# Folding layer 2's DFT over columns twice, in a two-layer FNet and GLU kernel

## The chip, the core and the metric

The kernel runs on one core of one Trainium2 chip. The metric is the device time of one execution in microseconds (us), as the median of the runs shown. Engines are named as the profile names them: PE (TensorE matmuls), PEld (its weight loads), DVE (VectorE), ACT (ScalarE), POOL (GpSimd), SP (SyncE, which issues nearly all DMAs here).

## The reference

Four sublayers run one after the other on 2048 rows of 640 columns, in float32; the same two sublayers twice:

```python
def _A_ref(x, dft_seq_re, dft_seq_im, dft_hid_re, dft_hid_im):
    a = jnp.einsum("bsd,ed->bse", x, dft_hid_re)
    b = jnp.einsum("bsd,ed->bse", x, dft_hid_im)
    return jnp.einsum("ts,bse->bte", dft_seq_re, a) - jnp.einsum("ts,bse->bte", dft_seq_im, b)

def _B_ref(x, w_gate, w_up, w_down):
    g = jnp.einsum("bsd,df->bsf", x, w_gate)
    u = jnp.einsum("bsd,df->bsf", x, w_up)
    return jnp.einsum("bsf,fd->bsd", _sigmoid(g) * u, w_down)

x = A_x
x = x + _A_ref(_layernorm(x), ...)
x = x + _B_ref(_layernorm(x), B_w_gate, B_w_up, B_w_down)     # F = 1728
x = x + _A_ref(_layernorm(x), ...)
x = x + _B_ref(_layernorm(x), B_w_gate, B_w_up, B_w_down)
```

The Fourier tables are inputs, so the kernel may use their symmetries only if it tests on the chip that they have them.

## The kernel before, in words

All rows of x stay in SBUF. Wherever precision matters a float32 value is cut into two float16 parts, a high part (ACT, `activation` with Copy) and a residue (DVE), by `split`; a product is then three matmuls: high with high, high with low, low with high (`PASSES`).

**The Fourier part.** Rows lie in four quads (`GA` to `GD`), so that rows s, S - s, S/2 - s and S/2 + s stand in one place. `fold_columns` adds and subtracts column c and column 640 - c, into an even part `fe` of 321 columns (`EC`) and an odd part `fo` of 320 (`EH`). `fold_rows` applies the layer norm and folds two rows onto each other; `fold_join` joins the four quads into the sums for even (`EV`) and odd (`OD`) output rows and cuts them into parts "e" and "o". `sequence(i, tp)` is one step of 18 matmuls, the DFT over rows for quad i and parity tp, into three PSUM banks (three column tiles, `KT`: 128, 128 and 65 columns). `evict_sums` cuts these sums into the parts `z`. `hidden(q, ph)` and `hidden_middle` are the DFT over columns: `product` runs three matmuls for each of three tiles and both tables (18 in all), with 321 columns of the table `h` moving each time. Two banks hold its result. `evict_hidden` brings them out, `combine`, `join_hidden` and `add_hidden` unfold them and add them to x. The sequence step of layer 2 is called "he" (its first step's index), and "b0" is the first step of the gate block that follows.

**The gate blocks and the down products.** `gate_up` multiplies normalised and transposed rows by the gate and up weights (L1130). The later tiles use a scheme with seven products instead of eight (`seven`, `four`: L1174); the down product does likewise in seven stages (`stage`, `rest_stage`: L1430, L1411), and layer 1's first half runs plainly (`down`: L1316). The rows of a second half are prepared by `pair_apply`, `pair_combine`, `pair_parts` and DMA transposes (`pair_transpose`, L533).

**The tests.** `load_rows` and `test_rows` (and others like them, for columns and for the hidden tables) load 512 KB of a table into one of three rooms, fold it on DVE (L1509, L1511) and sum the squares on ACT (`square_rest`, L1481). 100 such tests are spread over the run: test n loads room n mod 3 at its slot, folds it two slots later, and squares 0.85 slots after that. The flag that they give decides at the end whether a general kernel has to run instead.

**The order.** `steps` is the list of PE's steps with planned lengths. `when(t, f)` puts a job ahead of the step that holds the planned time t; `run(u, ...)` puts jobs ahead of step u. Each engine then does its instructions in the order of issue. SBUF room is given by a fixed list of places (`PLACES`), one for each `take`; the eight PSUM banks go round in the order in which they are freed.

## Time and profile before

| | us |
|---|---|
| median of 3 runs | 1104.65 |
| lowest, highest | 1103.58, 1104.69 |
| profiled execution, own time | 1106.03 |
| its span | 1104.2 |
| PE busy | 1084.0 |
| DVE busy | 830.2 |
| ACT busy | 572.9 |
| POOL busy | 154.6 |

The profile is of one execution. Its span runs from the first to the last instruction; the execution's own time has a little around it. A group of the profile gives line, engine, operation, tiles and shape, how often it ran, its busy time and the mean length of one, and what ended the idle time of its engine before it. Matmuls are pipelined, so the listed length of one matmul is longer than the distance from one to the next; that distance is read from the length of a merged piece.

### The profile page before, as it was taken

What the parts mean: (1) busy time and instruction counts of PE and PEld (TensorE: products, weight loads), DVE (VectorE), ACT (ScalarE), POOL (GpSimd) and SP (SyncE); (2) the same over time, 40 slices, a digit from 0 to 9 for tenths busy, and PEclk for the clock granted to TensorE, in tenths of its full rate; (3) what the DMA queues carried; (4) which work ended last, traced back from release to release, by engine and by line L of the source; (5) the groups of instructions that cost most, each with busy time, mean ns of one, the idle gap of its engine ahead of it and who ended that gap; (6) DMA issues with size and microseconds to landing.
All of it is one profiled execution on the core that took longest, in us unless ns stands there. A gap on an engine that the chain in (4) does not pass through costs nothing.

```text
span 1104.2 us, 17528 instructions
## 1 busy us (share of the span) xinstructions
PE 1084.0 (98%) x6289; PEld 626.3 (57%) x6289; DVE 830.2 (75%) x1608; ACT 572.9 (52%) x1109; POOL 154.6 (14%) x250
## 2 busy tenths in 40 slices
PE   6999999999999999999999999999999999999997
PEld 3776444457774444457777844444677444444775
DVE  8996789868448999769887569895895356777962
ACT  7776547765315665555225544476761345555520
POOL 3110153312333151000110100012000010000010
PEclk9999999999999999999999999999999999999999
DMA  8414765366996877756742058645569856666521
GB/s 273 155 61 71 199 184 203 115 193 191 251 249 233 251 250 202 235 174 214 229 141 73 1 62 194 200 154 182 185 163 177 265 180 208 202 196 194 190 88 64
DMA packets 183079, 194.70 MB, mean 176 GB/s; under 512 B 76451, under 2 KB 145474, under 8 KB 182982
## 3 DMA queue, kind: packets, MB, share of 16 engines
q1 hardware_dynamic: 182342, 190.87, 58.8%
q0 software_dynamic: 640, 2.62, 0.6%
q8 instruction: 51, 0.84, 0.3%
q14 instruction: 46, 0.38, 0.1%
HBM read 145.29 MB, written 31.91 MB: 160 GB/s over the span
## 4 chain that ended last, share of the span: by engine, by line
PE 87%; DVE 8%; issue 2%; DMA 1%; ACT 1%; POOL 0%; SPq 0%; DVEq 0%; POOLq 0%; ACTq 0%
PE acc L1174 36%; PE acc L1430 17%; PE acc L1130 14%; PE acc L1316 8%; PE acc L922 4%; PE acc L1411 2%; PE acc L1283 2%; PE acc L834 2%; DVE big L642 1%; DMA big<-big 1%; DVE quad L424 1%; DVE big L239 1%; PE acc L796 1%; DVE big L1509 1%; DVE big L594 0%
## 5 line engine op out<-in xcount | busy, mean ns | idle before, releaser
L1174 PE MATMUL acc<-big 128*128 128x512 f16 x2160 | 467.8, 379 | 2.8 <-ACT big L1178 1.9
L1174 PEld LDWEIGHTS <-big 128*128 128x128 f16 x2160 | 211.3, 98 | 257.8 <-issue 3.5
L1430 PE MATMUL acc<-big 128*128 128x320 f16 x1512 | 213.2, 299 | 0.4 <-DVE big L1304 0.4
L1178 ACT ACTIVATE big<-acc 128x512 f32<-128x512 f32 x160 | 94.0, 593 | 191.9 <-PE acc L1174 167.5
L1430 PEld LDWEIGHTS <-big 128*128 128x128 f16 x1512 | 147.9, 98 | 58.5 <-issue 0.6
L1130 PE MATMUL acc<-big 128*128 128x512 f16 (+1 forms) x900 | 156.6, 336 | 0.0
L1130 PEld LDWEIGHTS <-big 128*128 128x128 f16 x900 | 87.9, 98 | 67.7 <-DVE big L239 0.2
L1481 ACT ACTIVATE big<-big 128x768 f32<-128x768 f32 (+6 forms) x106 | 79.0, 745 | 53.2 <-DVE big L1511 17.0
L1304 DVE SCALAR_TENSOR_TENSOR big<-acc,big 128x320 f32<-128x320 f32 x112 | 53.1, 485 | 53.7 <-PE acc L1411 27.2
L239 DVE SCALAR_TENSOR_TENSOR big<-big 128x640 f16<-128x640 f32 (+7 forms) x94 | 75.9, 830 | 22.5 <-ACT big L237 19.4
L1316 PE MATMUL acc<-big 128*128 128x320 f16 x656 | 89.3, 299 | 0.0
L1391 DVE TENSOR_TENSOR big<-big 128x512 f16<-128x512 f32 x126 | 85.3, 688 | 2.3 <-ACT big L1390 2.3
L1390 ACT ACTIVATE big<-big 128x512 f16<-128x512 f32 x126 | 74.0, 618 | 25.0 <-DVE big L1391 11.1
L237 ACT ACTIVATE big<-big 128x640 f16<-128x640 f32 (+9 forms) x94 | 63.8, 707 | 35.7 <-POOL big L1082 15.8
L1316 PEld LDWEIGHTS <-big 128*128 128x128 f16 x656 | 64.2, 98 | 25.1
L1224 DVE TENSOR_TENSOR big<-big,acc 128x512 f32<-128x512 f32 x40 | 27.3, 682 | 44.4 <-PE acc L1174 30.6
L516 ACT ACTIVATE big<-big 128x384 f16<-128x384 f32 (+2 forms) x56 | 36.0, 667 | 36.6 <-DVE big L501 17.2
L1181 ACT ACTIVATE big<-big 128x512 f32<-128x512 f32 x80 | 49.7, 622 | 9.7 <-DVE big L1224 6.6
L386 POOL DMA_INDIRECT out<-big,rows x8 | 8.6, 1070 | 310.9 <-DVE big L1304 173.5
L1509 DVE TENSOR_TENSOR big<-big 128x512 f32<-128x512 f32 x64 | 46.2, 722 | 5.9 <-DMA big<-in_ct 5.7
L1402 DVE TENSOR_TENSOR big<-big 128x512 f32<-128x512 f32 x72 | 50.1, 697 | 0.1
L439 POOL TENSOR_SCALAR rowt<-rowt 128x1 f32<-128x1 f32 x24 | 13.0, 540 | 242.4 <-ACT big L437 242.4
(199 smaller groups left out, 1230.2 us busy)
## 6 DMA issues: line engine op xcount, KB each, us to landing
big<-in_ct SPq DMA_DIRECT2D x256, 128.0 KB
big<-kept_f SPq DMA_DIRECT2D x63, 320.0 KB
big<-kept_S SPq DMA_DIRECT2D x33, 512.0 KB
big<-kept_w SPq DMA_DIRECT2D x33, 320.0 KB
big<-in_ct SPq DMA_DIRECT2D x32, 256.0 KB
big<-kept_G SPq DMA_DIRECT2D x21, 320.0 KB
kept_S<-big SPq DMA_DIRECT2D x13, 512.0 KB
big<-in_wg SPq DMA_DIRECT2D x19, 320.0 KB
```

Of the source, the lines that this page charges most:

```text
L237: nc.scalar.activation(dh, src, AF.Copy, scale=s)
L239: nc.vector.scalar_tensor_tensor(dl, src, s, dh, op0=OP.mult, op1=OP.subtract)
L1130: nc.tensor.matmul(ps, w[wp][:, d * P : (d + 1) * P], xt[:, xp, :], start=(d == 0 and wp == HI and xp == HI), stop=(d == ND - 1 and wp == LO))
L1174: nc.tensor.matmul(ps, wt, xt, start=start and n == 0, stop=n == len(todo) - 1, skip_group_check=not start)
L1178: nc.scalar.activation(dst, ps, AF.Copy)
L1304: nc.vector.scalar_tensor_tensor(xe, ps[:, :EH], CB, xe, op0=OP.mult, op1=OP.add)
L1316: nc.tensor.matmul(held["pd", i, e][0][:, :EH], held["t", half, j].parts[hp][:, i * P : (i + 1) * P], held["w", 2, j].parts[wp][:, e * EH ...
L1390: nc.scalar.activation(h, v, AF.Copy)
L1391: nc.vector.tensor_tensor(l, v, h, op=OP.subtract)
L1430: nc.tensor.matmul(ps[:, :EH], a[n][hp][:, i * P : (i + 1) * P], w[n][:, wp], start=fresh and m == 0, stop=m == len(todo) - 1, skip_group_ ...
L1481: nc.scalar.activation(v, v, AF.Square, accum_out=new_sum()[:p])
L1509: nc.vector.tensor_tensor(bd[:, :, 1], bd[:, :, 0], bd[:, :, 1], op=same)
```

## The change

**Layer 2's DFT over columns is folded once more.** In layer 2 (`steps` not empty) `fold_columns` and `fold_double` put the even part's columns in order 0 to 320. `fold_join` has a stage more, `fold_again`: it adds column k and column 320 - k (318 - k for the odd part) for the outputs of one parity and subtracts them for the other, 161 and 160 columns. The tiles of the DFT over rows (`KT2`) are then set so that a tile of 128 columns belongs to outputs of one parity: the first two tiles of a table move 161 columns each, into two halves of a bank, and the third, of 65, moves 322. `evict_hidden` and `evict_middle` read the two halves alternately and so write the outputs in their natural order.

**The tables.** Layer 1's tables are no longer stored and loaded again. `load_wh2` loads the rows that are wanted from the input early in layer 1's last down product, and `split_wh2` cuts them, with every second column and with new factors (`hs2`, eleven small DVE operations at the start).

**The order of the layer change.** `sequence(3, EV)` comes ahead of `sequence(2, OD)`; `hidden(0, 1)` follows `hidden(0, 0)`; the middle step comes ahead of the last two. `fold_join` of quad 3 is cut by parity and set between the evictions.

**The tests.** Six tests are added, for the second fold (106 in all). They are spread by other spans, each with a distance of its own: none in layer 2's first down product, some from 10 us after b0, one in 2.9 us in the last gate block, where there are four rooms and a fold comes three slots after its load.

**Others.** The last two rows of layer 2's second half are prepared 4 and 5 us earlier. Scales `XF` and `ZS` are halved. All `PLACES` are new.

```diff
@@ KT
-    KT = (((0, P), (P, P), (2 * P, EC - 2 * P)),) * 2
+    KT = (0, P), (P, P), (2 * P, EC - 2 * P)
+
+    KT2 = (0, P), (EC - P, P), (P, EC - 2 * P)
@@ fold_columns, fold_double
+    def doubled():
+        return 0 if steps else EH
...
-        nc.vector.tensor_tensor(e[:, :, :EH], a, b, op=OP.add)
+        c = int(doubled() == 0)
+        nc.vector.tensor_tensor(e[:, :, c : c + EH], a, b, op=OP.add)
@@ fold_again, fold_join
+    def fold_again(to, f, r):
+
+        c, every = EH - 2 * r, (slice(None),) * (len(f.shape) - 1)
+        for n, to_c, op in ((HE + 1, 0, OP.add), (HE, HE + 1, OP.subtract)):
+            nc.vector.tensor_tensor(to[(*every, slice(to_c, to_c + n))], f[(*every, slice(0, n))],
+                                    f[(*every, slice(c, c - n, -1))], op=op)
...
             if 0 in do:
-                for g, op in zip((GB, GD), ops):
-                    nc.vector.tensor_tensor(f[:, g], f[:, GA], f[:, GC], op=op)
+                for k in only:
+                    nc.vector.tensor_tensor(f[:, GB + 2 * k], f[:, GA], f[:, GC], op=ops[k])
...
             if 1 in do:
-                nc.scalar.activation(take_parts(key, i)[:, :, 0, :w], f[:, GB::2], AF.Copy)
-                if n:
-                    nc.gpsimd.memset(take_parts(key, i)[:, :, :, EH : EH + 1], 0.0)
+                fold_again(a, b, n)
             if 2 in do:
-                p = take_parts(key, i)
-                nc.vector.tensor_tensor(p[:, :, 1, :w], f[:, GB::2], p[:, :, 0, :w], op=OP.subtract)
+                nc.scalar.activation(p[:, :, 0, :EC], a, AF.Copy)
+            if 3 in do:
+                nc.vector.tensor_tensor(p[:, :, 1, :EC], a, p[:, :, 0, :EC], op=OP.subtract)
...
@@ the tables
-    def load_wh_again(r, d):
-        v = take(3, "h", r, d).f16.rearrange("p (q c) -> p q c", q=2)
-        nc.sync.dma_start(v[: KT[r][d][1], :, :EC], kept["h", r, d])
+    def load_wh2(r, d):
+        s = take(3, "hr", r, d).f32
+        for p, row, n in (((0, r, P),), ((0, 32 + r, P),), ((0, P + r, 33), (33, r, 32)))[d]:
+            nc.sync.dma_start(s[p : p + n, :EC], wh[r, row : row + n, :EC])
+
+    def split_wh2(r, d, do=ALL):
...
@@ product
-        for d, (_, n) in enumerate(KT[r]):
-            w = held["h", r, d].f16[:n]
+        for d, (_, n) in enumerate(KT):
+            o = ps[:m, : EC + 1 if steps else EC]
+            if steps and d < 2:
+                c = (r + d) % 2
+                o = ps[:m, c * (HE + 1) : (c + 1) * (HE + 1)]
+            ws = [w[:n, : o.shape[1]] for w in held["h", r, d].parts]
...
-                    nc.tensor.matmul(ps[:m, :EC], z[:, at : at + m], w[:, 384 * wp : 384 * wp + EC],
+                    nc.tensor.matmul(o, z[:, at : at + m], ws[wp],
...
@@ evict_hidden
+    def sums_of_bank(ps):
+        return ps[:, : EC + 1].rearrange("p (h k) -> p k h", h=2) if steps else ps[:, :EC]
...
-                nc.scalar.activation(v[:, n], ps[:, :EC], AF.Copy, scale=CY)
+                nc.scalar.activation(in_order(v[:, n]), sums_of_bank(ps), AF.Copy, scale=CY)
...
@@ order of layer 2's steps
-                     (sequence, 2, OD), (hidden, 0, 0), (sequence, 3, EV), (hidden, 1, 0), (sequence, 3, OD),
-                     (hidden, 0, 1), (hidden, 2, 0), (hidden, 3, 0), (hidden, 1, 1), (hidden, 2, 1), (hidden, 3, 1),
-                     (hidden_middle,)]
+                     (sequence, 3, EV), (sequence, 2, OD), (hidden, 0, 0), (hidden, 0, 1), (sequence, 3, OD),
+                     (hidden, 1, 0), (hidden, 1, 1), (hidden, 2, 0), (hidden, 3, 0), (hidden_middle,),
+                     (hidden, 2, 1), (hidden, 3, 1)]
@@ jobs of the layer change
-    run(he + 2, evictions(0, (EV,)))
+    join = [[(fold_join, 3, ALL, (n,), (k,)) for n in range(1, 4)] for k in range(2)]
+    run(he + 2, [(evict_sums, 0, EV, 0), (fold_join, 3, ALL, (0,)), *join[0], *evictions(0, (EV,))[1:], *join[1]])
     run(he + 4, evictions(0, (OD,)))
...
@@ rows of layer 2's second half
-            u = d0 + ((2, 20, 47, 57) if first else (6, 20, 46, 56))[i]
+            u = d0 + ((2, 20, 47, 57) if first else (6, 18, 42, 51))[i]
@@ tests
-        tests.insert(30 + 4 * n, test)
-    spans = [(start_of(0, "d", 0) + 6, start_of(0, "d", 0) + 38, 0.4), (start_of(0, "d", 0) + 76, start_of(0, "e"), 0.55),
-             (start_of(1, "c", 1, 0) + 5, start_of(1, "j", 0, JC), 0.7), (start_of(1, "j", 0, JC), start_of(1, "d", 0) - 7, 1.0),
-             (start_of(1, "d", 0) + 6, start_of(1, "d", 0) + 58, 0.45),
-             (start_of(1, "j", 1, 0), start_of(1, "j", 1, 0) + 50, 0.6),
-             (start_of(1, "j", 1, 0) + 50, start_of(1, "d", 1), 1.1), (start_of(1, "d", 1), start_of(1, "d", 1) + 30, 0.6)]
-    pace = sum((b - a) * w for a, b, w in spans) / len(tests)
+        tests.insert(18 + 4 * n, test)
+    d, c, j = (start_of(0, "d", 0), start_of(0, "d", 1)), start_of(1, "c", 1, 0), start_of(1, "j", 0, JC)
+    d2, j2, e2 = start_of(1, "d", 0), start_of(1, "j", 1, 0), start_of(1, "d", 1)
+    spans = [(d[0] + 6, d[0] + 38, 7.0), (d[0] + 76, d[1] - 93, 14.0), (d[1] - 43, d[1] - 3, 5.0), (d[1] - 3, d[1] + 47, 12.0),
+             (c - 29, c + 14, 4.5), (c + 14, c + 58, 11.0), (c + 58, d2 - 4, 4.8),
+             (j2 + 4, e2, 2.9), (e2, e2 + 45, 5.5)]
```

More of the change, by code (lines that the diff above doesn't have):

```diff
@@ L947, in drop_hidden @@
             for d in range(3):
-                if ("h", r, d) not in kept:
-                    keep(held["h", r, d].f16.rearrange("p (q c) -> p q c", q=2)[: KT[r][d][1], :, :EC], "h", r, d)
                 drop("z", r, d)
@@ L1769, in folded @@
     run_at(t + 5, [(fold_rows, 2, k, ALL, (1,)) for k in range(2)])
-    for n in range(3):
-        when(t + 8 + 3 * n, fold_join, 2, ALL, (n,))
+    for n in range(4):
+        when(t + 8 + 2.5 * n, fold_join, 2, ALL, (n,))
     for k in range(2):
@@ L1986, in folded @@
         when(at_test(22 + 8 * r), test_edges, r)
[L1987 to L1988 removed]
+    more_rooms = next(n for n in range(len(tests)) if at_test(n) >= j2 + 4)
+    for k in range(4):
+        when(at_test(k if k < 3 else more_rooms) - 0.2, take, CK, "room", k)
     for n, (load, test, key) in enumerate(tests):
[L1990 to L1995 removed]
+        m = n - more_rooms
+        k, wait = (n % 3, 2) if m < 0 else ((3, *((more_rooms + i) % 3 for i in range(3)))[m % 4], 3)
+        when(at_test(n), within, k, load, *key)
+        when(at_test(n + wait), within, k, test, *key)
+        when(at_test(n + wait + 0.85), square_rest)
+    for k in range(4):
+        when(at_test(len(tests) + 3.9), drop, "room", k)
+    when(at_test(len(tests) + 4), test_all)
     for u, (_, mm, post) in enumerate(steps):
```

169 lines of the change are left out of this document (107 added, 62 removed), and 64 rows, old and new, of the table PLACES.

## The prediction

> **What bounds the kernel now.** I read the page's engine table first, then what PE waited for, then the chain that ended last, and then the timelines of the layer change.
>
> ```profile
> span 1104.2 us, 17528 instructions
> PE 1084.0 (98%) x6289; PEld 626.3 (57%) x6289; DVE 830.2 (75%) x1608; ACT 572.9 (52%) x1109; POOL 154.6 (14%) x250
> PE acc L1174 <- ACT big L1178: 1.9, 1, 1.9
> PE acc L1174 <- DMA big<-big: 0.9, 1, 0.9
> PE acc L796 <- DVE big L239: 0.6, 1, 0.6
> PE acc L922 <- ACT big L971: 0.5, 1, 0.5
> ```
>
> PE is busy in 1084.0 of 1104.2 us. After the opening it waits for little: the four waits shown make 3.9 us. So the time is the columns that PE streams, plus these waits, plus any that the change adds. A saving on another engine is worth nothing unless one of these waits is its doing.
>
> ```profile
> 584.68 2.46 PE acc L922 x18
> 587.15 1.97 PE acc L796 x18
> 619.18 1.12 PE acc L540 x20
> 779.84 12.22 PE acc L1430 x90
> 850.82 9.21 DMA big<-big
> 860.07 149.73 PE acc L1174 x693
> 571.66 2.47 PE L796 MATMUL acc<-big 128*128 128x257 f16 x21
> 612.46 6.71 PE L1130 MATMUL acc<-big 128*128 128x256 f16 x60
> ```
>
> The first six are pieces of the chain (start, length), the last two of PE's timeline. Layer 2's Fourier part runs from 571.66 to 612.46: eight `sequence` steps at 1.97 us and nine hidden steps at 2.46 us, plus the transposes and two waits.
>
> **The columns that PE loses.** A hidden step is 18 matmuls of 321 columns, 2.46/18 = 137 ns each. The change leaves six of them at 322 columns and cuts twelve to 161. The nearest shorter row is the transposes: 128 columns, a weight load before each, 1.12/20 = 56 ns. On the line between 56 ns at 128 and 137 ns at 321, 161 columns take 70 ns. A step becomes 6 x 0.137 + 12 x 0.070 = 1.66 us; nine steps save 9 x 0.80 = 7.2 us. Bounds of one matmul: 56 ns below, 137 ns above (no gain at all); I take 70, since the near row is 33 columns away.
>
> The row of the transposes speaks of back-to-back pairs of weight load and matmul at 128 columns. [...]
>
> **The layer change, step by step.** What PE saves counts only if DVE and ACT keep up there. The rows:
>
> ```profile
> 576.90 1.02 DVE L642 SCALAR_TENSOR_TENSOR big<-big,quad 128x321 f32<-128x321 f32 x2 [0.79 <-ACT big L636]
> 577.84 1.69 DVE L675 TENSOR_TENSOR big<-big 128x321 f32<-128x321 f32 x4
> 579.60 1.65 DVE L682 TENSOR_TENSOR big<-big 128x642 f16<-128x642 f32 x2
> 581.16 3.67 DVE L239 SCALAR_TENSOR_TENSOR big<-acc,big 128x512 f16<-128x512 f32 x6
> 598.31 1.56 DVE L1009 TENSOR_TENSOR big<-big 128x642 f32<-128x642 f32 x2
> 580.29 2.99 ACT L237 ACTIVATE big<-acc 128x512 f16<-128x512 f32 x6
> 601.65 1.40 ACT L971 ACTIVATE big<-acc 128x321 f32<-128x321 f32 x4
> 607.84 0.74 ACT L437 ACTIVATE big<-big 128x640 f32<-128x640 f32 x1
> 609.53 0.75 ACT L971 ACTIVATE big<-acc 128x321 f32<-128x321 f32 x2
> L1511 DVE TENSOR_TENSOR big<-big 128x128 f32<-128x128 f32 x128 | 32.8, 298 | 2.2
> ```
>
> One eviction is 0.60 us on DVE (3.67/6) and 0.49 on ACT; four joins 1.69. A new half fold (161 elements, two operands) lies between L1511 at 128 elements and a join at 321: about 0.33 us alone, 0.25 to the next. Quad 3 needs eight, so DVE gets 2.0 us more. I lay the new order out by hand from 577.9, when L642 ends as before (nothing ahead of it changes in that stage).
>
> DVE: one eviction to 578.6, four joins to 580.2, the first half's folds to 581.2, its two residues to 582.2. PE ends `sequence(2, EV)` at 581.8 and `sequence(3, EV)` needs the last residue in its second half, so it hardly waits and ends at 583.8. DVE: two evictions to 583.5, the other half's folds and residues to 585.5, then the first odd eviction to 586.2. `sequence(2, OD)` takes its third bank from that eviction and wants it at 585.1: PE waits 1.05 us. Hidden (0,0) from 586.9, (0,1) to 590.2, `sequence(3, OD)` to 592.2, (1,0) and (1,1) to 595.5: banks are free. Hidden (2,0)'s second bank comes from the last three evictions, which stand on ACT behind the statistics of row 1: bank free at 597.2, PE wants it at 596.3, so 0.9 us. Hidden (3,0), middle, (2,1) to 603.0, transposes to 604.2. Hidden (3,1) takes the banks of (2,1), whose eviction stands on ACT behind the statistics of row 3, as the middle step's did at 609.53 behind L437: free at 605.4, so 1.2 us. PE then starts the gate block at about 607.2, where it was 612.46: **-5.3 us**. That is 7.2 saved, the old waits of 1.1 gone, 3.1 of new ones. Bounds: -8.3 (no waits left) and -2.7 (below). The rows 2 and 3 that are normalised for the gate block's second part are due at 613.7 and ready near 611.7 by the same count, so they hide.
>
> New ACT and DVE reads of the hidden sums take the two halves of a bank alternately, a stride of 161 floats. No row of before reads PSUM so. Lower bound: no extra, by L971 (0.35 us for 321). Upper: twice the element time, +0.3 us each on 14 ACT and 4 DVE reads, of which the count above passes on 2.6 us to 609.8, hence the -2.7. I take no extra, since L1511 reads a strided half in SBUF at 298 ns for 128, on the line with the joins' 1.69/4 at 321.
> [...]
>
> **The other moves.** Rows of the chain's end, of SP and DVE, and of five stretches (their columns: length, then the busy time of PE, weight loads, DVE, ACT and POOL, PE's clock, DMA share, GB/s):
>
> ```profile
> 837.06 11.89 SPq L533 DMA_TRANSPOSE big<-big  x1
> 850.82 7.16 SPq L533 DMA_TRANSPOSE big<-big  x1
> 876.80 2.60 SPq L1502 DMA_DIRECT2D big<-in_ct  x4
> L1502 SPq DMA_DIRECT2D big<-in_ct x256: 588/597/2972, 251.6 to 989.2; - x128
> L1509 DVE TENSOR_TENSOR big<-big 128x512 f32<-128x512 f32 x64 | 46.2, 722 | 5.9 <-DMA big<-in_ct 5.7
> 613.00:650.00 37.00, 37.00 (x275) 25.85 (x274) 21.99 (x44) 16.54 (x30) 1.48 (x3) 1.00 0.19 31
> 385.00:432.00 47.00, 45.10 (x210) 20.35 (x209) 46.59 (x80) 28.46 (x52) 17.38 (x23) 1.00 0.70 229
> 857.00:910.00 53.00, 52.10 (x248) 24.10 (x247) 23.02 (x43) 20.94 (x42) 4.19 (x4) 1.00 0.69 222
> 910.00:960.00 50.00, 50.00 (x234) 22.62 (x232) 35.18 (x69) 27.30 (x57) 0.00 (x0) 1.00 0.59 195
> 960.00:1018.00 58.00, 58.00 (x270) 26.32 (x269) 41.81 (x84) 29.90 (x63) 0.00 (x0) 1.00 0.63 201
> ```
>
> The transpose issued at 850.82 lands at 860.03 and PE's wait of 0.9 us hangs on it alone. The change applies that pair 5 us earlier and the one before 4 us earlier, and takes the tests out of that stage: **-0.9 us**. Bounds -0.9 and 0.
>
> In 385 to 432 DVE is busy 46.59 of 47 us, and ACT's L1178 there started behind a join of quad 1 (1.9 us of PE). The tests in layer 1's second gate block and the stage before come every 14 us or not at all instead of every 8.1 (the old plan: spans times weights give 445.4 us for 100 tests, at weight 0.55): six fewer up to there. Each is 0.72 us of L1509 and two L1511, about 1.25 us. That is 7.5 us off DVE against 1.9 for the folds of quad 0 and some of quad 1's: **-1.9 us**. Bounds -1.9 and 0; I take the whole since DVE ran only some 5 us behind.
>
> In the last gate block the tests go from 33 (50 us at weight 0.6 and 108 at 1.1, over 4.45) to 53 (154 us at one each 2.9). SP: four loads of a row test take 2.60 us, so three row tests, one of the short kind (1.1) and the weights of one block (1.3) make 10.2 of 11.65 us. DVE has 100.0 busy us of 161 in the three rows from 857 to 1018; 20 more tests at about 1.2 us make 124. DMA there is at 195 to 222 GB/s; 20 loads of mostly 512 KB in 154 us add some 50. PE has no wait after the 0.9 in these rows; the nearest stretch with a crowded DVE, 385 to 432, had 1.9 us in 47. So between 0 and 6.2 (that rate over 154 us); I take **+0.5**, as DVE stays at 77%.
>
> Layer 1's change of nothing but scales, the 11 tiny DVE operations at the start (the DVE has idle time before its first x tiles) and six stores fewer: 0. The six tables, now loaded from the input and split on ACT and DVE during layer 1's last stages, add eight DVE operations of about 0.3 us; two to three tests leave the same 50 us, which covers them. If that cover were gone, PE would wait 2.4 us at most. The layer change's tests, ten of 1.25 us from 10 us into the gate block, fit in what 613 to 650 leaves (DVE 21.99 of 37 busy).
>
> Sum against the profiled execution, 1106.03 us (span 1104.2, so 1.8 around it): 1106.0 - 5.3 - 0.9 - 1.9 + 0.5 = 1098.4. The median of before, 1104.65, stands 1.4 below its profiled execution, so the forecast for the median is **1097.0**.
>
> **The rivals.** (1) The alternating PSUM reads cost double: gate block at 609.8, 1099.6. For: no two neighbours in a read. Against: strided SBUF reads show nothing.
> (2) Matmuls of 161 columns run at the weight load's pace: at the 98 ns that a load is listed with for 128 columns, 9 x 12 x 28 ns = 3.0 us less, 1100.0 at most, partly swallowed by the new waits.
>
> ```profile
> L540 PEld LDWEIGHTS <-big x80: 95/98/98, 66.7 to 620.0; 128*128 128x128 f16 x80
> ```
>
> Against: the same loads went by at 56 ns each in the transposes.
> (3) Slower: SP falls behind in the last gate block. It has 1.45 us to spare in 11.65. If a load's issue takes 0.85 us instead of 0.6 (the longest of all is 2.97), twelve of them add 3.0 us, SP loses 1.6 us in each of 13 blocks, 21 us in all; the weights are issued 15 us ahead and need some 5 to land, so PE waits for the last 11 us: 1108. It decides from about 0.73 us, where nothing is left to spare. For: the block's DMAs and DVE tests hang on each other through the rooms. Against: the median issue is 0.597 us, and four rooms let a load start early.
> (4) No change worth measuring: the layer change is set by DVE and ACT altogether and the last block gives back 2 to 3 us: 1103.
>
> **How the numbers follow.** My forecast (1094 to 1099) has 0.55, (1) 0.15, (2) 0.08, (3) 0.10, (4) 0.12. Range 1094.0 to 1103.5: the low end is all waits of the layer change gone, the high end takes in (1), (2) and (4), and leaves (3) and a little below out. Within 0.2% (2.2 us) means 1102.4 to 1106.9, about what a measurement of this kernel can tell from no change: (4) and a piece of (3), 0.12; slower 0.09; faster 0.79.
>
> **What would show it.** In the changed kernel's lines: twelve of 18 hidden matmuls at 161 columns and a pace near 70 ns; eight half folds of about 0.33 us after the joins; the gate block's first L1130 35.5 us after the first L796 (now 40.8); no wait of PE for the transposes near 860 - 8 and none for L1178 near 428; evictions of the hidden sums still 0.35 us apart on ACT. It is wrong if PE waits more than 4 us in the layer change, or if waits of L1174 for weights or for ACT appear in the last gate block.

## The result, and the profile after

| | median, us | runs from, to | profiled execution | span | mean granted clock |
|---|---|---|---|---|---|
| before | 1104.67 | 1103.58 to 1106.23 (4) | 1106.03 | 1104.2 | 0.998 |
| after | 1136.28 | 1135.01 to 1141.0 (4) | 1141.0 | 1139.2 | 0.985 |

The changed kernel is slower: ratio 1.0293, 95% interval 1.0259 to 1.0327. The forecast was 1097.0. Both profiles are of executions above their medians, after's by 4.7 us (the longest of its four) and before's by 1.4, so they differ by 35.0 us where the medians differ by 31.6.

The page of after, its engine table:

```profile
span 1139.2 us, 17670 instructions
PE 1089.1 (96%) x6289; PEld 625.1 (55%) x6289; DVE 842.6 (74%) x1663; ACT 575.6 (51%) x1131; POOL 147.1 (13%) x254
```

What PE waited for in it (total, times, longest):

```profile
PE acc L1237 <- ACT big L1241: 22.7, 10, 5.6
PE acc L1237 <- DMA big<-kept_G: 5.5, 1, 5.5
...
PE acc L1237 <- DVE big L1574: 1.7, 1, 1.7
...
PE acc L1193 <- ACT big L1544: 0.9, 1, 0.9
```

L1237 is the matmul of the later gate blocks and L1241 the eviction that follows it (L1174 and L1178 before); L1193 is that of layer 2's first gate_up. PE has lost columns, yet it is busy 5 us longer and its share has fallen from 98 to 96%: it waits, and beside some of the waits its granted clock is halved for 3 to 10 us.

Where in the kernel? The first matmul of each stage in PE's timeline gives the stages' lengths in us. The experiments' rows stand here as well.

| kernel | layer 1, 2nd gate block | its stage | layer change | layer 2, 1st gate block, two parts | its stage | last gate block | last stage |
|---|---|---|---|---|---|---|---|
| before | 160.0 | 79.9 | 40.8 | 79.2 + 88.1 | 80.4 | 158.0 | 79.5 |
| after | 158.4 | 80.0 | 34.8 | 86.1 + 93.1 | 79.3 | 190.1 | 79.5 |
| e1_even | 164.7 | 81.9 | 35.1 | 79.2 + 88.3 | 80.9 | 158.0 | 79.5 |
| b1_plan (on before) | 158.0 | 79.8 | 40.8 | 80.0 + 88.1 | 79.3 | 203.4 | 80.8 |
| p1_clear_change | 163.3 | 81.4 | 34.8 | 79.2 + 88.1 | 79.3 | 195.1 | 80.7 |
| e2_half_loads | 159.9 | 91.9 | 34.8 | 94.0 + 93.6 | 79.3 | 269.3 | 79.5 |
| e3_pool_loads | 162.1 | 80.8 | 34.8 | 90.4 + 90.9 | 79.3 | 177.6 | 79.5 |
| e4_thin_tests | 158.0 | 79.3 | 34.8 | 85.3 + 92.9 | 79.3 | 185.6 | 79.5 |
| e5_thin_loads | 158.0 | 79.5 | 34.8 | 82.6 + 92.8 | 79.3 | 165.1 | 79.5 |
| e6_thin_sixteen | 158.0 | 79.6 | 34.8 | 81.9 + 92.8 | 79.3 | 165.3 | 79.5 |
| e7_full_sixteen | 158.9 | 79.9 | 34.8 | 82.1 + 93.4 | 79.3 | 170.1 | 79.5 |
| e8_all_sixteen | 158.1 | 79.3 | 34.8 | 80.5 + 88.1 | 79.3 | 158.0 | 79.5 |
| b2_plan | 160.0 | 79.3 | 34.8 | 79.2 + 91.3 | 81.0 | 163.0 | 80.9 |
| b3_mixed | 162.9 | 79.3 | 34.8 | 79.1 + 88.1 | 79.7 | 158.0 | 79.5 |
| b4_mixed | 158.4 | 80.3 | 34.8 | 79.1 + 88.3 | 79.3 | 159.9 | 85.3 |
| b5_mixed | 158.9 | 81.9 | 34.8 | 79.1 + 90.0 | 82.0 | 158.0 | 79.5 |

After minus before: -1.6 in layer 1, -6.0 in the layer change, -1.1 at the transposes, then +11.9 in layer 2's first gate block and +32.1 in the last one. Together +35.3, against 35.0 by the spans. All that was to be won was won (8.7 us, forecast 8.1), and in this execution 44 us were lost where the tests went.

The last gate block as one window of before, and the group of its matmuls (the window: length, busy us of PE, weight loads, DVE, ACT and POOL, PE's clock, DMA share as a mean over 16 engines, GB/s; the group: count, busy us, mean ns, idle time before them):

```profile
860.00:1018.00 158.00, 157.93 (x732) 71.61 (x732) 99.22 (x192) 78.14 (x161) 4.19 (x4) 1.00 0.63 205
L1174 PE MATMUL acc<-big 128*128 128x512 f16 x702 | 151.8, 379 | 0.9 <-DMA big<-big 0.9
```

The same window of after:

```profile
863.00:1053.00 190.00, 167.22 (x734) 73.29 (x732) 115.17 (x244) 90.20 (x197) 4.87 (x4) 0.96 0.63 203
```

The waits in it, and the group of its matmuls:

```profile
ACT big L1544 <- DVE big L1574: 55.2, 16, 6.1
DVE big L1572 <- DMA big<-in_ct: 42.5, 18, 5.1
...
PE acc L1237 <- ACT big L1241: 22.4, 9, 5.6
DVE big L1644 <- DMA big<-in_wh: 13.9, 6, 3.8
```

```profile
L1237 PE MATMUL acc<-big 128*128 128x512 f16 x702 | 161.2, 392 | 22.8 <-ACT big L1241 22.4 <-DMA big<-kept_w 0.4
```

Read the waits from the transfers up. DVE stands 42.5 us for the row tests' loads (L1572) and 13.9 for the hidden folds' (L1644). Behind it ACT stands 55.2 us, since it meets a test's square (L1544) in its queue before the next eviction; and behind ACT, PE stands 22.4 us for that eviction, 22.8 in all. No engine is full (DVE 115 of 190 us), and the DMA share is 0.63, no more than before. A share of 0.63 looked like room. The other 9.3 us of the 32.1 go with PE's lower clock: 167.2 us busy for the work of 157.9. The granted clock stands at one half in four stretches, 17.1 us in all, each of them beside a wait of 2.8 to 5.6 us; the longest:

```profile
917.41:924.24 6.83, 5.51 (x14) 1.93 (x14) 3.13 (x8) 4.35 (x11) 0.00 (x0) 0.50 0.65 211
```

The chain of after, in order of time (start, length), in one block:

```profile
931.94 8.48 DMA big<-kept_S
940.43 0.60 SPq L1565
...
943.76 5.23 DMA big<-in_ct
949.02 0.70 DVE big L1572
949.75 0.19 DVE big L1574
949.94 7.80 DMA big<-in_ct
957.80 0.60 SPq L1565
```

And SP's timeline there, the twelve row loads of a block:

```profile
933.00 11.37 SPq L1565 DMA_DIRECT2D big<-in_ct  x12
```

A row load of 128 KB takes 5.23 us to land, a load of weights 8.48, and the row load at 940.43 goes out only when the weights issued at 931.94, eight transfers before, have landed: SP's queue is held up too. In the trace each load on SP's queue raises the same semaphore as the eighth before it (780 of 780), and in the whole last gate block 81 of 203 loads go out only at that one's landing, 32.8 us of holding in all. What makes these loads late is the question: theory N, the number of transfers under way on SP's queue; theory E, how many of the 16 DMA engines a load uses, which it supposes to follow from the first number of its pattern (8 in `[[256, 8], [d * S, 16], [1, 256]]`); or theory W, the tests' work on DVE and ACT.

### The profile page after: what moved, and what is told of

The parts are those of the page before. It is cut to its first block, busy times and chain, and to the rows that moved or that the text cites. A ratio compares the mean times of both kernels' runs of the same rounds, so it can differ in the third digit from the quotient of the medians.

```text
span 1139.2 us, 17670 instructions
## 1 busy us (share of the span) xinstructions
PE 1089.1 (96%) x6289; PEld 625.1 (55%) x6289; DVE 842.6 (74%) x1663; ACT 575.6 (51%) x1131; POOL 147.1 (13%) x254
## 4 chain that ended last, share of the span: by engine, by line
PE 68%; DMA 13%; DVE 12%; ACT 2%; SPq 2%; issue 2%; POOL 0%; DVEq 0%; ACTq 0%
PE acc L1237 27%; PE acc L1493 15%; PE acc L1193 8%; PE acc L1379 8%; DMA big<-in_ct 7%; DMA big<-kept_U 3%; PE acc L976 2%; PE acc L1474 2%; PE acc L1346 2%; PE acc L863 2%; SPq L1565 1%; DMA big<-kept_S 1%; DVE big L241 1%; DMA big<-in_x 1%; DVE big L1465 1%
## 5 line engine op out<-in xcount | busy, mean ns | idle before, releaser
L1237 PE MATMUL acc<-big 128*128 128x512 f16 x2160 | 480.3, 385 | 30.2 <-ACT big L1241 22.7
L1237 PEld LDWEIGHTS <-big 128*128 128x128 f16 x2160 | 213.5, 99 | 295.6 <-issue 39.1
L1241 ACT ACTIVATE big<-acc 128x512 f32<-128x512 f32 x160 | 92.3, 589 | 145.0 <-PE acc L1237 140.6
L1193 PE MATMUL acc<-big 128*128 128x512 f16 (+1 forms) x900 | 156.8, 336 | 1.0 <-ACT big L1544 0.9
L1544 ACT ACTIVATE big<-big 128x768 f32<-128x768 f32 (+7 forms) x112 | 81.4, 726 | 128.8 <-DVE big L1574 67.0
L1193 PEld LDWEIGHTS <-big 128*128 128x128 f16 x900 | 87.9, 98 | 69.2 <-issue 1.4
L241 DVE SCALAR_TENSOR_TENSOR big<-big 128x640 f16<-128x640 f32 (+9 forms) x97 | 75.6, 802 | 17.6 <-ACT big L239 17.5
L239 ACT ACTIVATE big<-big 128x640 f16<-128x640 f32 (+11 forms) x97 | 64.6, 695 | 35.9 <-POOL big L1145 11.1
L1453 ACT ACTIVATE big<-big 128x512 f16<-128x512 f32 x126 | 73.1, 616 | 11.5 <-DVE big L1331 7.7
L1572 DVE TENSOR_TENSOR big<-big 128x512 f32<-128x512 f32 x64 | 43.9, 687 | 46.9 <-DMA big<-in_ct 46.5
L1244 ACT ACTIVATE big<-big 128x512 f32<-128x512 f32 x80 | 49.7, 621 | 11.9 <-DVE big L1287 7.9
L526 DVE TENSOR_TENSOR big<-big 128x384 f16<-128x384 f32 (+2 forms) x56 | 41.9, 756 | 6.8 <-ACT big L525 6.5
L448 POOL TENSOR_SCALAR rowt<-rowt 128x1 f32<-128x1 f32 x24 | 10.2, 424 | 259.0 <-ACT big L446 258.9
```

The lines of the kernel that those rows point to most:

```text
L239: nc.scalar.activation(dh, src, AF.Copy, scale=s)
L241: nc.vector.scalar_tensor_tensor(dl, src, s, dh, op0=OP.mult, op1=OP.subtract)
L1193: nc.tensor.matmul(ps, w[wp][:, d * P : (d + 1) * P], xt[:, xp, :], start=(d == 0 and wp == HI and xp == HI), stop=(d == ND - 1 and wp == LO))
L1237: nc.tensor.matmul(ps, wt, xt, start=start and n == 0, stop=n == len(todo) - 1, skip_group_check=not start)
L1241: nc.scalar.activation(dst, ps, AF.Copy)
L1453: nc.scalar.activation(h, v, AF.Copy)
```

## The experiments

The ratios are to before on the same chip, with 95% intervals.

**Is it the plan of the tests?** `e1_even` is the changed kernel with the tests at the old kernel's spans and weights, in three rooms; `b1_plan` is the old kernel with the new distances from layer 2 on (wider ones in layer 1, since it has six tests fewer), in three rooms.

```diff
# e1_even, against after (shortened)
+    old = [..., (start_of(1, "j", 1, 0), start_of(1, "j", 1, 0) + 50, 0.6),
+           (start_of(1, "j", 1, 0) + 50, start_of(1, "d", 1), 1.1), ...]
...
-        when(at_test(n), within, k, load, *key)
+        when(at_even(n), within, n % 3, load, *key)
# b1_plan, against before (shortened)
+    plan = [...,
+            (c - 29, c + 14, 4.5), (c + 14, c + 58, 11.0), (c + 58, d2 - 4, 4.8),
+            (j2 + 4, e2, 2.9), (e2, e2 + 45, 5.5)]
...
-        when(at_test(n), within, n % 3, load, *key)
+        when(at_plan(n), within, n % 3, load, *key)
```

> The changed kernel with its 106 tests spread by the old kernel's spans and weights (three rooms in use, a fold two slots after its load); all else as in the changed kernel. Theory A (the places of the tests are the whole loss; the double fold, the new order and the earlier rows are a gain of 9 us, as the marks of the two traces say: 1.9 in layer 1's gate block, 6.0 in the layer change, 1.0 at the last DMA transposes): 1094 to 1098 us. Rival theory R1 (the new SBUF places or the other new order cause a good part of the waits): over 1105 us.

> The kernel before, with its 100 tests at the changed kernel's distances (4.5 us from 10 us after the gate block's start, 2.9 us in the last gate block; three rooms); nothing else of the change. Theory A: 25 to 50 us slower than before, 1130 to 1155, with PE's waits in the last gate block behind ACT's squares and with the layer change as before. Rival R1: within 10 us of before.

e1_even: 1107.72 us (1106.54 to 1109.43), ratio 1.003 (1.0018 to 1.0043). b1_plan: 1153.25 us (1150.27 to 1154.74), ratio 1.0444 (1.0428 to 1.046). The plan alone, put on the old kernel, makes its last gate block 45.4 us longer and nothing else by more than 1.3. Layer 2's first gate block, too, takes only 0.8 us more there, though the new distances hold in it; which tests stand in it differs (43 row loads and no hidden ones from 610 to 691 us of b1_plan, 31 and 4 from 604 to 691 of after). With the old plan, the changed kernel's two late gate blocks are back at 158.0 and 79.2 + 88.3 and the layer change keeps 35.1. But the sum isn't the forecast, and e1_even's expected time was missed: the old plan costs 6.3 us more in layer 1's second gate block than the new one and 1.9 in its stage, and so hands back there what the folds save. It is also 4.7 us more in that block than in before, with the same plan. There e1_even has four loads of hidden tests (11.5 us from issue to landing, the median) and before none; what else the six tests more and the new places do there was not told apart.

```profile
PE acc L1237 <- ACT big L1241: 5.6, 5, 1.4
...
PE acc L1493 <- DVE big L1367: 3.5, 4, 1.2
```

These are e1_even's waits of PE; the five of L1237 all lie between 360 and 450 us, in layer 1.

**The tests of the layer change elsewhere.** `p1_clear_change` puts the tests due in layer 2's first gate_up into layer 1's second gate block.

```diff
# after's spans, and the plan in their place (shortened)
-             (d[0] + 76, d[1] - 93, 14.0), ..., (c - 29, c + 14, 4.5),
+             (d[0] + 76, d[1] - 93, 8.2), (d[1] - 93, d[1] - 43, 8.8), ...
```

> The changed kernel, but the ten tests that it puts around 10 to 53 us after the gate block's start go into layer 1's second gate block instead; the last gate block stays crowded. Theory A: the 11.3 us that the first half of the layer 2 gate block lost (605 to 695 took 90.4 us instead of 79.2) come back, the 32 of the last gate block stay: 1123 to 1127 us. Rival R1: near 1136.

1141.9 us (1140.73 to 1143.67), ratio 1.0337 (1.0321 to 1.0353). Layer 2's first gate block goes back to 79.2 + 88.1, all of its 11.9, so that loss too is those tests; but layer 1 takes 4.9 and 1.4 more and the last gate block 5. The expected time was missed: the same tests cost 6.3 us in layer 1, and why the last gate block takes 5 us more stays open.

**Fewer transfers, the same bytes.** `e2_half_loads` brings the rows of a test in two loads of 256 KB in place of four of 128 KB.

```diff
-        for g, (row, d) in enumerate(((s, 1), (S - s, -1), (HS - s, -1), (HS + s, 1))):
-            ... [[256, 8], [d * S, 16], [1, 256]]
+        for g, (row, d) in enumerate(((s, 1), (S - s, -1))):
+            ... [[512, 4], [d * S, 32], [1, 512]]
```

> The changed kernel, but a row test loads two pieces of 128 x 512 instead of four of 128 x 256: as many bytes, half the DMAs; it compares other rows, its two small folds and its square run over 512 columns, so it does not test all that is needed. Theory A1 (SP lets only eight DMAs be on their way, so 17 DMAs in 11.65 us are too many at 5 to 8 us each from issue to landing; eleven are not): the last gate block falls from 190 us to 158 to 163, the whole to 1096 to 1112. Rival B (the bytes of the tests are too many for the DMA engines): no gain, 1130 to 1140. Rival D (the DVE and ACT work of a test every 2.9 us is too much): no gain beyond 3 us, as that work is nearly the same.

1245.36 us (1243.57 to 1248.7), ratio 1.1276 (1.1253 to 1.1298). Half the transfers, and over four times the loss. The chain between 988 and 1036 us:

```profile
988.61 12.34 DMA big<-in_ct
1001.04 0.70 DVE big L1570
...
1020.56 13.89 DMA big<-in_ct
1034.54 0.70 DVE big L1570
```

A load of twice the bytes lands after 12.3 to 13.9 us, where after's chain had 5.2 and 7.8. So the number of transfers under way is not what is short. What changed besides is the first number of the pattern: 4 pieces of 512 columns in place of 8 of 256.

**The queue, the work, or the bytes.** Three variants of after: `e3_pool_loads` issues the row loads from POOL's queue; `e4_thin_tests` loads all but tests 128 of each 256 columns; `e5_thin_loads` also loads only those 128.

```diff
# e3_pool_loads
-            nc.sync.dma_start(v[:, g], ... [[256, 8], [d * S, 16], [1, 256]])
+            nc.gpsimd.dma_start(v[:, g], ...)
# e4_thin_tests
-        nc.vector.tensor_tensor(bd[:, :, 1], bd[:, :, 0], bd[:, :, 1], op=same)
+        nc.vector.tensor_tensor(bd[:, :, 1, :128], bd[:, :, 0, :128], bd[:, :, 1, :128], op=same)
...
# e5_thin_loads, besides
+            nc.sync.dma_start(v[:, g, :128], ... [[256, 8], [d * S, 16], [1, 128]])
```

> The changed kernel with its row loads issued from POOL's queue in place of SP's, all else as it was. In the last gate block POOL is busy for under 5 us of 155, so it has the time. Theory N (each queue lets only eight transfers be under way, and SP's own loads of weights stand behind the test loads): SP keeps its 4 or 5 loads in 11.65 us, the last gate block goes from 190 back to 158 to 166 us and the first half of layer 2's gate block from 179 to 167 to 172; in all 1094 to 1112 us. Theory E (a row load has 8 as its slowest dimension and so uses 8 engines, the four loads of a test the same ones, and the landing is set by the bytes on these): the loads still take about 5 us or more to land and DVE, in order, still waits for them; part of the loss stays: 1110 to 1130 us. Theory W (the tests' work on DVE and ACT is too much for the place): no gain, 1130 to 1140 us.

> The changed kernel with every row load as it was, but only 128 of each 256 loaded columns compared, folded and squared (the other half isn't tested): DVE's and ACT's work for a row test is nearly halved, the transfers are the same. Theory W: the last gate block goes to under 168 us, in all under 1114 us. Theories N and E: it stays at 180 to 190, in all 1126 to 1138 us.

> As the kernel with thin tests, and the row loads bring only those 128 of 256 columns: as many transfers, half their bytes (64 KB in place of 128 KB). Against the kernel with thin tests only the bytes differ. Theory E (landing by bytes per engine): the loads land in about 3 us in place of 5.2, the last gate block goes to 158 to 170 us, in all 1094 to 1115 us. Theory N as it stands (number of transfers alone, each with a fixed time): within 5 us of the kernel with thin tests. Theory W: the same as the kernel with thin tests, and that one under 1114 us.

e3: 1136.16 us (1133.42 to 1139.41), ratio 1.029 (1.0251 to 1.0328). e4: 1136.89 (1134.07 to 1139.13), ratio 1.0295 (1.0257 to 1.0333). e5: 1111.07 (1109.69 to 1116.86), ratio 1.0066 (1.0046 to 1.0085).

Nearly half of the row tests' work on DVE and ACT taken away changes nothing in the total (e4; 4.5 us of the last gate block), so theory W falls as the main cause. Half the bytes, with as many transfers, win 26 us (e5), so theory N falls in its plain form. On POOL's queue the last gate block gains 12.5 us, but layer 1's loses 3.7 and the first part of layer 2's 4.3, and the total stays: missed by both theories that expected a gain. (It lies where theory W put it, which e4 speaks against.) From the page of e3, the row loads' time from issue to landing:

```profile
big<-in_ct POOLq DMA_DIRECT2D x256, 128.0 KB, 6.4
```

What DVE waited for in its last gate block:

```profile
DVE big L1572 <- DMA big<-in_ct: 38.4, 10, 12.5
```

With a queue of their own the loads still take 6.4 us to land (median), and DVE still waits 38.4 us for them. So the queue is at most a part of it, the 12.5 us; that the loads land late is not its doing.

**The engines of a load.** `e6_thin_sixteen` is e5 with 16 as the first number of the row loads' pattern. `e7_full_sixteen` is after with full loads, the same in number, bytes and packets of 1 KB, from 16 overlapping pieces (it tests 8 of every 16 rows, some columns twice). `e8_all_sixteen` also does it to the hidden tests' loads, where that number was 2.

```diff
# e6_thin_sixteen, against e5
-            ... [[256, 8], [d * S, 16], [1, 128]]
+            ... [[128, 16], [d * S, 8], [1, 128]]
# e7_full_sixteen, against after
-            ... [[256, 8], [d * S, 16], [1, 256]]
+            ... [[112, 16], [d * S, 8], [1, 256]]
# e8_all_sixteen, besides
-            ... [[EH, 2], [d * D, 64], [1, EH]]            ... [[HE, 2], [d * D, n], [1, HE + 1]]
+            ... [[10, 16], [d * D, 8], [1, EH]]            ... [[4, 16], [d * D, n // 8], [1, HE + 1]]
```

> As the kernel with thin loads (four loads of 64 KB a test in packets of 512 B, 128 columns compared), but each load takes 8 rows of 16 pieces of 128 columns in place of 16 rows of 8 pieces: its slowest dimension is 16 in place of 8, so by theory E it uses 16 engines in place of 8. Number of transfers, bytes, packets and the work on DVE and ACT are the same (it tests other elements, and half of them). Theory E with shared engines: the loads land sooner, and the last gate block goes from 165.1 to 158 to 161 us, the first half of layer 2's gate block from 175.4 to 167 to 173; in all 1096 to 1105 us. Rival (only the bytes as a whole matter, not on how many engines they lie): within 3 us of the kernel with thin loads, 1108 to 1114.

> The changed kernel with its plan, its number of loads, their full 128 KB and packets of 1 KB; only each row load now takes 16 overlapping pieces of 256 columns (112 apart) from 8 rows in place of 8 pieces from 16 rows, so its slowest dimension is 16 (it tests 8 of every 16 rows, and some columns twice). Work on DVE, ACT and SP is the same. Theory E: on 16 engines in place of 8 the loads land sooner; DVE no longer waits for row loads but still for the hidden folds' loads, whose slowest dimension is 2; last gate block from 190 to 160 to 172 us, in all 1100 to 1120. Rival (bytes and their packets as such, on however many engines; the kernel with thin loads on 16 engines was no faster than that on 8): last gate block 180 to 192, in all 1128 to 1140.

> As the kernel with full row loads on 16 engines, and the loads of the hidden tests changed in the same way: 16 overlapping pieces of as many columns as before from 8 rows (4 in the last fold) in place of 2 pieces from 64 rows, so 16 is their slowest dimension in place of 2; as many loads and bytes, packets as long, the same work on DVE, ACT and SP (they test fewer rows, and some columns several times). Theory E for all of the loss: last gate block from 170.1 to 158 to 163 us, layer 2's first gate block from 175.5 to 167 to 171, in all 1094 to 1106. Rival (what is left comes from how densely the tests stand: work on DVE and ACT, issue on SP): last gate block 167 to 171, in all 1112 to 1118.

e6: 1109.54 us (1107.78 to 1111.76), ratio 1.0039 (1.0023 to 1.0054). e7: 1117.28 (1116.32 to 1118.67), ratio 1.0105 (1.0078 to 1.0132). e8: 1097.87 (1097.76 to 1098.7), ratio 0.9941 (0.9927 to 0.9956).

DVE's waits for transfers in the last gate block of e6:

```profile
DVE big L1572 <- DMA big<-in_ct: 15.9, 11, 2.8
DVE big L1644 <- DMA big<-in_wh: 14.8, 5, 4.5
```

And of e7:

```profile
DVE big L1572 <- DMA big<-in_ct: 25.7, 10, 3.7
...
DVE big L1644 <- DMA big<-in_wh: 9.0, 4, 3.3
```

e6 came out as the rival had it, within 2 us of e5; but nearly half of what DVE waited for there were the hidden folds' loads, whose pattern still began with 2. e7 takes 20 us off the last gate block with nothing altered but the row loads' pattern, and e8 the other 12. The window of e8's last gate block:

```profile
858.00:1016.00 158.00, 158.00 (x751) 73.22 (x750) 119.11 (x250) 91.43 (x200) 4.51 (x4) 1.00 0.80 249
```

The group of its matmuls there:

```profile
L1237 PE MATMUL acc<-big 128*128 128x512 f16 x675 | 146.0, 379 | 0.0
```

PE's waits in e8 from 600 to 800 us:

```profile
PE acc L1193 <- DMA big<-big: 0.9, 1, 0.9
PE acc L976 <- ACT big L1032: 0.5, 1, 0.5
```

One block's row loads on SP:

```profile
929.92 8.17 SPq L1565 DMA_DIRECT2D big<-in_ct  x12
```

The same 53 tests, DVE busier than in after, 39 MB moved (158 us at 249 GB/s; after 190 at 203, also 39), and PE's matmuls stand idle for 0.0 us. SP needs 8.17 us for these twelve loads, where after took 11.37 (7.6 to 10.0 in e8's blocks, 9.8 to 12.6 in after's). DVE's wait for the row loads, 42.5 us in after, is down to one:

```profile
DVE big L1572 <- DMA big<-in_ct: 0.9, 1, 0.9
```

So the two losses of 44 us come from the loads' patterns, all but 1.3 us of them. The profile lists no single engine, only their mean. But the traces keep each rise of a load's semaphore from its issue to its landing. For a row load there are 9 in before (256 of 256) and after (253), 5 in e2 and 16 in e6, e7 and e8; for a hidden load whose pattern begins with 2 there are 3 (20 of 20 in before), and 16 in e8 (a few loads of some traces show fewer). That is one more than 8, 4 and 2, or 16; theory E takes it for the number of engines. The same records give the time from issue to landing in the last gate block, as medians in us:

| | row load | hidden fold's load | weights kept_S |
|---|---|---|---|
| after | 6.2 | 7.0 | 7.6 |
| e2 | 13.8 | 13.3 | 8.5 |
| e7 | 3.8 | 5.1 | 7.3 |
| e8 | 3.4 | 2.3 | 5.0 |

Loads whose pattern stayed as it was land sooner too (the hidden folds' in e7, the weights in e8). In before a row load took 5.4 us, hardly less than in after; but before has 79 of them in 158 us, and after 127 in 190.

The traces keep each packet's start and length as well, and so how many are moved at once. In after, over the stretches in which nothing is under way but

- four or more loads of weights (18.6 us), 15.75 packets are moved at once in the mean;
- seven or eight row loads (31.0 us), 7.55;
- three or more row loads and one or two hidden ones whose patterns begin with 2 (14.3 us), 7.71.

Two such hidden loads alone have 1.54 (before, 10.7 us). So the row loads, even eight of them, move as much at once as eight engines would, and the hidden loads beside them add nothing: they share, as theory E has it. Which engines they are, no run shows. The stages agree: 190.1 us with 8 and 2 as the first numbers of row and hidden loads, 170.1 with 16 and 2, 158.0 with 16 and 16, and 269.3 with 4 and 2. An estimate from these counts and the packet times in after's last gate block (row loads 806 us over eight engines, hidden folds 53 over two of the same, all else 1049 over sixteen) has two engines busy for 193 of its 190 us and eight others for 66; in e8, if all sixteen are alike, the share of 0.80 makes 126 of 158 for each. It is rough, but it shows how a mean share of 0.63 can hide engines that have no room.

e7 and e8 also read fewer rows of the tables, parts of them twice. That this made the bytes cheaper is not what the traces show: a packet of 1 KB took 50 ns in after's last gate block (the mean), 56 in e7's and 55 in e8's. Loads of the very same elements with 16 as the first number weren't tried, so a direct test of that stays open.

**A plan that beats both.** `b2_plan` spreads the tests (3.82 us in the last gate block, none in layer 2's first gate_up). `b3_mixed` also mixes them: from layer 2 on, one column test, whose loads begin with up to 128 rows (and raise their semaphore 16 times, all 32 of them in after), and one hidden test for every two row tests. `b4_mixed` and `b5_mixed` shift densities.

```diff
# b2_plan, the last of after's spans and the plan in their place (shortened)
-             (j2 + 4, e2, 2.9), (e2, e2 + 45, 5.5)]
+             (d2 + 6, d2 + 58, 8.5), (j2 + 4, e2, 3.82), (e2, e2 + 45, 4.6)]
# b3_mixed (b4: 14.0, 11.0, 3.2; b5: 12.0, 10.5, 3.33, hidden tests from the 19th on)
+    (d[0] + 76, d[1] - 93, 9.0), ..., (d2 + 6, d2 + 58, 13.0), (j2 + 4, e2, 3.4), (e2, e2 + 45, 5.4)
-        tests.insert(18 + 4 * n, test)
+        for q in ((0, 1, 2)[n % 4 == 3],) if n < 29 else ((0, 2, 0, 1)[n % 4],):   # 0 row, 1 hidden, 2 column
+            tests.append(next(k for k in (kinds[q], by_row, by_col, more) if k).pop(0))
```

> The changed kernel with its tests spread anew: 3.8 us apart in the last gate block in place of 2.9 (40 in place of 53 by the plan), none in layer 2's first gate_up, 4.0 in place of 4.8 in the gate block's second half, 8.5 apart in layer 2's stage (none before), 7.8 in place of 14 in the early part of layer 1's second gate block (its late part stays free, where the even spread waited), and the end 6 us later. If the loss is only that the test loads stood too densely (all of E, N and W): last gate block 158 to 166 us, first half of layer 2's gate block 167 to 170, layer change 35; in all 1094 to 1104 us. If 3.8 us is still too dense: 1105 to 1120 us, with the wait of L1237 for ACT L1241 left in the last gate block.

> The changed kernel with its tests mixed anew as well as spread: row tests and hidden tests in layer 1, as the changed kernel has them (row tests every 9 us in the early part of the second gate block), and from layer 2's gate block on one column test (two loads with 128 partitions as the slowest dimension, so 16 engines by theory E) and one hidden test for every two row tests; 3.4 us apart in the last gate block, so a row test about every 6.8 us in place of every 3.9. Theory E: last gate block 158 to 163 us though the tests stand nearly as close as in the changed kernel, layer 2's gate block 167 to 169, layer change 35, layer 1's second gate block 158 to 160; in all 1094 to 1102 us. Theory N or the density of tests as such: last gate block over 168 us, in all over 1106 us.

> The kernel with mixed tests, with layer 1's second gate block as sparse as in the changed kernel (14 us between tests in its early part, in place of 9; there the mixed kernel took 162.9 us and the changed one 158.4), and the tests taken out of it put into the last gate block (3.2 us apart in place of 3.4) and layer 2's stage. If column and hidden tests between the row tests leave room in the last gate block: layer 1's block 158 to 160, the last one 158 to 161, in all 1095 to 1100 us. If 3.4 us was already the limit there: the last gate block 164 or more, in all 1101 to 1110.

> The kernel with mixed tests, spread anew: row tests alone at first, hidden tests among them only from the 19th test on (with hidden tests from the 4th on, the two mixed kernels took 1 to 2 us more ahead of layer 1's second gate block), column tests lasting to the end, layer 1's early part 12 us apart, the last gate block 3.33. If the densities between the two mixed kernels are right: layer 1's second gate block 158 to 161, the last 158 to 159, the end 79.5, in all 1096 to 1101 us. If one of them is over its limit: 1101 to 1108.

b2: 1108.54 us (1105.72 to 1111.39), ratio 1.0032 (1.0018 to 1.0046). b3: 1101.2 (1099.18 to 1102.34), ratio 0.9963 (0.995 to 0.9977). b4: 1108.42 (1106.48 to 1111.3), ratio 1.0027 (1.0014 to 1.004). b5: 1103.8 (1099.97 to 1107.29), ratio 0.9995 (0.9982 to 1.0008). The window of b3's last gate block:

```profile
856.50:1014.50 158.00, 158.00 (x734) 71.65 (x733) 111.93 (x230) 86.00 (x182) 4.71 (x4) 1.00 0.69 223
```

At 3.4 us between tests the block costs nothing once row tests alternate with others, where b2 at 3.82 and mostly row tests took 163.0; b2 came out in its second case, with 2.5 us of L1237's waits for L1241 left there. b3 makes every test and came within its expected time. It is 0.4% faster than before (interval 0.2 to 0.5%) and some 35 us faster than the changed kernel. It still loses 4.5 us to after in layer 1's second gate block; b4 and b5 won these back and lost more elsewhere (b4 5.8 in the last stage, b5 2.6 and 2.3 in two stages), so the times that they were made for were missed. Why those places lost stays open.

## Why the prediction was wrong, step by step

**The columns: right.** Forecast 1.66 us for a hidden step and 70 ns for 161 columns. In after, two steps are one piece of the chain:

```profile
585.04 3.35 PE acc L976 x36
```

1.675 us a step; with 6 x 137 ns taken off, 71 ns each for the other twelve. Rival 2 (98 ns) falls.

**The layer change: right, and low by 0.7 us.** Forecast -5.3, measured -6.0, with the three foreseen waits at 0.8, 0.8 and 0.5 in place of 1.05, 0.9 and 1.2:

```profile
PE acc L825 <- DVE big L241: 0.8, 1, 0.8
PE acc L976 <- DVE big L241: 0.8, 1, 0.8
PE acc L976 <- ACT big L1032: 0.5, 1, 0.5
```

The alternating reads, by after's groups of lines:

```profile
L1032 ACT ACTIVATE big<-acc 128x322 f32<-128x322 f32 x12 | 4.5, 447 | 0.3 <-PE acc L976 0.2
L684 DVE TENSOR_TENSOR big<-big 128x161 f32<-128x161 f32 x4 | 1.3, 319 | 0.0
```

And the same eviction in before:

```profile
L971 ACT ACTIVATE big<-acc 128x321 f32<-128x321 f32 x24 | 9.0, 431 | 2.9 <-PE acc L922 2.9
```

They cost next to nothing: 447 ns for 322 elements read alternately, 431 for 321 in a row, 16 ns more for the whole read. So rival 1 (twice the element time) falls, and with -6.0 us rival 4's layer change that is set by DVE and ACT. A half fold takes 319 ns (forecast 0.33 us).

**The transposes and layer 1: right.** -1.1 (forecast -0.9) and -1.6 in the gate block (-1.9).

**The last gate block: wrong by 31.6 us, and this is the step that failed.** The prediction put +0.5, with 0 to 6.2 as bounds, and measured was +32.1. Its own sign of being wrong came: PE's waits for ACT in this block. It priced SP by the time of an issue, DVE by its busy time and the transfers by their mean rate, found room in each, and left out how long a load takes to land when its few engines are shared by all loads of its kind. The warning stood in its own rows: "20 loads of mostly 512 KB in 154 us add some 50" (GB/s) stood as the whole price, but a row load took 6.2 us to land, a hidden one 7.0, and DVE, ACT and at last PE waited for them. The upper bound came from a stretch where DVE's work was the limit (46.59 of 47 us busy), so it couldn't bound this.

**The tests of the layer change: wrong by 11.9.** "fit in what 613 to 650 leaves" counted DVE's time alone (21.99 of 37 us). Of the 11.9, 8.1 are three waits of PE, and the rest goes with a granted clock of one half for 10.2 us beside them. The largest wait is L1237's 5.5 us for the weights kept_G. SP's timeline ahead of it:

```profile
683.39 3.90 SPq L542 DMA_TRANSPOSE big<-big  x1
687.39 0.53 SPq L1166 DMA_DIRECT2D big<-kept_G  x1
```

DVE's, earlier (in brackets its idle time before, and for what):

```profile
655.38 0.49 DVE L1629 TENSOR_TENSOR big<-big 128x320 f32<-128x320 f32 x1 [9.91 <-DMA big<-in_wh]
```

The weights left SP at 687.39, behind transposes (L542) of what DVE makes, and DVE had fallen behind by waits such as the 9.91 us for a hidden test's load, on a pattern that begins with 2. That this one wait led to that one is argued from the order; what the runs show is that in e8, with 16 as the first number of these loads' patterns and as many tests, all but 1.3 us is gone, that e7, with the row loads alone changed, keeps 8.2, and that b1_plan, with row tests alone in this place, lost 0.8.

**Rival 3** named the place and the sign, slower by SP falling behind. Its trigger was a wrong one: a row load's issue stayed at 0.6 us in after (the piece at 940.43), SP fell behind only where it had to wait for landings, and PE waited for weights for 0.4 us in that block, for ACT's evictions for 22.4. Its price, 1108, was 28 us too low: it had 11 us of waits in that block, where there were 22.8, and nothing for the lower clock beside them (9.3) or for the first gate block (11.9).

With both losses gone, e8 took 1097.87 us, 6.5 less than before on the same chip, against a forecast of 1097.0 and 7.65 less: the other terms of the sum add up to about a microsecond.

## What to carry to other kernels

Price a transfer by what it takes from issue to landing beside the others of its kind, and look at the first dimension of its pattern before its bytes: loads that begin with 8, 4 or 2 pieces were late here (6.2, 13.8 and 7.0 us to landing), in after while the mean DMA share stood at 0.63. Look, too, at what stands behind background work in an engine's queue: here the chain (load, DVE, ACT, PE) turned 56 us of DVE's waits for loads into 55.2 of ACT's for DVE and 32 us of the kernel's time. Where the pattern can't be turned, mix such loads with others whose patterns begin with more, as b3 did (158.0 us for its last gate block).

## What the runs showed of the hardware beyond that

- A wait can cost more than its length: in after's last gate block 22.8 us of PE's waits came with 9.3 us of slower matmuls, at a mean granted clock of 0.96. Not each wait does: behind one of 2.8 us at 949 the clock stayed whole, beside one of 2.8 us at 982 it was halved for 3.4 us.
- SP's queue stopped until the eighth transfer before had landed (940.43 in after). In the last gate block that held 81 of 203 loads for 32.8 us in after, and 11 of 203 for 3.4 us in e8.
- DMA went to a share of 0.80 and 249 GB/s in e8's last gate block without one wait of PE; 0.63 and 203 GB/s in after's had ten.
